# Local attention and two layers on one core: a rational function in two passes, pooled queries by VectorE, larger packets, and Strassen's products in every group of layer two

## The chip, the cores and the metric

The kernel runs on one core of a Trainium2 chip. The metric is the device time of one execution in microseconds (us), the median over several runs; less is better. A core has five engines that work through their own queues: TensorE (PE, with its weight loads listed apart as PEld), VectorE (DVE), ScalarE (ACT), GpSimd (POOL) and SyncE (SP), from which this kernel issues all of its DMAs. Matrix products end in PSUM, eight banks of 512 float32 columns per partition; everything else lies in SBUF.

## The reference, cut to what matters

Attention over 2 x 8 heads of 576 positions and 64 columns has two parts that are added: a coarse one over means of four neighbours (144 positions), and a local one in which a position sees its neighbours at a distance under 4. Its result, 1152 tokens of 512 columns, passes through two layers of width 2048, and all is float32 in accuracy.

```python
q_d = q.reshape(B, H, Sd, factor, D).mean(axis=3)      # k_d, v_d alike, factor = 4
out_up = np.repeat(sm_attn(q_d, k_d, v_d), factor, axis=2)
out_local = softmax(scale * q @ k.T where |i - j| < factor) @ v
x = out_up + out_local                                  # as 1152 x 512

h = x @ w_in                                            # layer one: a rational function
P = a[0] + a[1] * h + a[2] * h**2 + a[3] * h**3
Q = 1.0 + abs(b[0]) * abs(h) + abs(b[1]) * h**2
x = (P / (Q + 1e-06)) @ w_out

h = x @ w_in2                                           # layer two: h * tanh(softplus(h))
return (h * np.tanh(log1p(exp(h)))) @ w_out2
```

The weights come as float64, 8 bytes an element, 32 pieces of 1 MB in all.

## The kernel before

Nothing in it is issued by hand: every piece of work is a task with a cost for each engine that may do it, a priority (a due time in us of planned PE time) and the buffers that it takes and uses. `Plan.run` plays the tasks through a model of the engines and writes each engine's queue in the order that comes out. `SECOND`, `FILL`, `LEAD`, `CLEAD`, `LLEAD`, `OLAG`, `PROL`, `PSTEP`, `VOFF`, `VROFF`, `LOFF` and `KOFF` set due times and when a second engine or a filler matmul (`warm`, L503) is chosen. On the chip each queue runs in that order, held by semaphores.

Attention comes in 18 units (`unit`), each four windows of 64 rows for one pair of heads, and in 8 preparations (`prep`), one for each pair of heads of a batch. `prep` loads keys, transposes them, sums four neighbours (`red`, L572, into kd) and loads values again (`vload`, L584, in runs of 1 KB) for the coarse sums `va` and `vb` (L590, L594). A unit loads queries (L618) and a window of values (L633). `pe_a` transposes the queries (L521) and multiplies them with a matrix `mean` (L645), which gives the pooled queries; `qcopy` (L660) brings both out of PSUM. `pe_b` (L679 to L692) gives the scores, and then come maxima (L704, L705), exponentials (L720, L728), sums (L733), the division (L742, L747), `pe_d` (L758, L763), `copy_p` (L773), `pe_e` (L788, L798), and the result x in two halves: a rounded one `xh` (L837) and the rest `xl` (L842).

Every product of the layers is done as three matmuls of such halves. Layer one works in three groups of 6, 6 and 4 slices of 128 hidden columns. A step is two slices for one chunk of tokens: four chunks in the first group, three of 384 (`TW`) in the others. It does H (L1113), 24 matmuls into two banks. ACT then makes three passes over H out of PSUM, `i_c` (L1133), `i_a` (L1138) and `i_b` (L1141); DVE makes `d_1` (L1148), `d_2` (L1151) and `d_3` (L1156). The quotient follows through Ln and Exp and a Newton step in the first group (L1171 to L1185), or through Ln and Sigmoid for pairs of steps in the others (`flush`, L1057 to L1073, and L1165). Then come the halves of g (L1211, L1216) and O (L1250), which sums in PSUM; `evac` adds that to `part` (L1342).

Layer two has four groups of four slices, two grains each, in pieces: "I" is H for one chunk (`plain`, L1489, 24 matmuls), "S" is H for chunks 1 and 2 together by Strassen's seven products (`seven`, L1433, 42 matmuls), and "O" (L1252, 18 matmuls) follows for a chunk. In the first group all three chunks are "I"; in the others chunk 0 is "I" and the rest "S". "S" needs sums of x (`sums`, L1291, with halves by `halves`, L1268 and L1273) and combinations of the weights: `combine` (L1027), `hi7` (L1031) and `lo7` (L1036), whose result lies in `late_r`, over memory that layer one's last groups use as well. Products p1 and p2 need neither sums nor combined weights.

Weights are decoded from float64 by `scale` (L969) and `low` (L976) on ACT and `join` (L983), `sign` (L989) on DVE, then split by `hi` (L995, L997) and `lo` (L1000). The float32 copy lies in one of two work tiles `wt` until the last of these, `lo7` included, is done.

```python
if m == 1 and kind == "i" and 2 * f >= GROUPS[1][0]:
    w7 = Buf(wT_s)
    ...
    y = add({"dve": 4 * t_dve(256)}, combine, c, after=[x], use=[src], port=True)
    y = add({"act": t_act(2 * DM), "dve": ...}, hi7, c, after=[y] + att_done, take=[w7], use=[src], ...)
```

## Time and profile before

| | |
|---|---|
| median of 3 runs | 487.15 us (486.61 to 492.02) |
| the profiled execution | 486.43 us |
| its span, from the first to the last instruction | 484.7 us |
| PE busy | 475.9 us, 98% |
| DVE busy | 361.2 us, 75% |
| ACT busy | 352.5 us, 73% |
| POOL busy | 55.8 us, 12% |
| HBM read and written | 44.17 MB and 2.36 MB |

The profile is one execution. Attention and layer one's first group fill about the first 130 us, layer one's other groups go on to some 300 us, and layer two ends it. Engine times are shares of the span, and matmuls are pipelined, so that a busy PE can still be waiting; how many matmuls stand in a stretch says more. The chain of waits follows the work that ended last back to the start, at each step to what released it. A wait for several semaphores is put down to the one that came last.

### The profile page before, as it was taken

The page shows a single profiled execution, that of the slowest core. Times are in us where ns is not written, and L with a number is a line of the kernel's source. Part 1 is how long each engine was busy: PE and PEld are TensorE (multiplying, and loading weights), DVE is VectorE, ACT ScalarE, POOL GpSimd, SP SyncE. Part 2 cuts the span into 40 slices and gives each one's busy share as a digit, 9 for nine tenths or more (in the row PEclk, how much of TensorE's full clock was granted, in tenths as well). Part 3 has the DMA queues.
Part 4 walks back from the last instruction along what each step waited for, and adds up shares of the span by engine and source line. Part 5 has one row for each costly group of instructions (what it writes and reads, how often), then busy time and mean ns, then how long its engine had stood idle before and what let it go on. Part 6 is the DMA issues. An engine that isn't in the chain of part 4 may idle for free.

```text
span 484.7 us, 9704 instructions
## 1 busy us (share of the span) xinstructions
PE 475.9 (98%) x4003; PEld 436.8 (90%) x4003; DVE 361.2 (75%) x528; ACT 352.5 (73%) x546; POOL 55.8 (12%) x79
## 2 busy tenths in 40 slices
PE   9989999999999999989999999999999999999996
PEld 5668898899999999989999999898988898889885
DVE  5647989985999988979799997909597759633332
ACT  6678989985899999999799977737667446422320
POOL 1835344644000000000000000000000000000000
PEclk9999999999999999999999999999999999999999
DMA  9868698741024024240312212120505220000103
GB/s 185 196 167 198 177 267 216 202 118 44 1 87 175 1 88 174 87 174 0 101 74 88 87 39 68 68 87 4 171 4 170 88 87 2 0 1 0 66 0 130
DMA packets 47132, 47.16 MB, mean 97 GB/s; under 512 B 30576, under 2 KB 33648, under 8 KB 47088
## 3 DMA queue, kind: packets, MB, share of 16 engines
q1 hardware_dynamic: 47088, 46.54, 32.8%
q8 instruction: 31, 0.51, 0.4%
q14 instruction: 13, 0.11, 0.1%
HBM read 44.17 MB, written 2.36 MB: 96 GB/s over the span
## 4 chain that ended last, share of the span: by engine, by line
PE 93%; ACT 4%; DMA 1%; SPq 1%; DVE 0%; issue 0%; ACTq 0%
PE psum L1250 20%; PE psum L1252 20%; PE psum L1113 20%; PE psum L1489 10%; PE psum L1433 9%; PE psum L503 2%; PE psum L798 2%; PE psum L521 2%; PE psum L686 2%; PE psum L692 1%; PE psum L788 1%; PE psum L645 1%; DMA att<-in_q_dram 1%; PE psum L758 1%; PE psum L763 1%; PE psum L679 1%
## 5 line engine op out<-in xcount | busy, mean ns | idle before, releaser
L1113 PE MATMUL psum<-xh,wi 128*128 128x384 f32 (+1 forms) x336 | 83.8, 320 | 1.2 <-ACT late_f L1141 1.2
L1250 PE MATMUL psum<-gg,wo 128*128 128x384 f32 (+1 forms) x456 | 71.9, 311 | 0.0
L1250 PEld LDWEIGHTS psum<-gg,wo 128*128 128x128 f32 x456 | 68.6, 189 | 0.5 <-ACT raw L976 0.2
L1113 PEld LDWEIGHTS psum<-xh,wi 128*128 128x128 f32 x336 | 59.1, 189 | 2.8 <-ACT late_f L1141 1.6
L1113 PE MATMUL psum<-xl,wi 128*128 128x384 f32 (+1 forms) x168 | 52.4, 312 | 0.0
L1252 PE MATMUL psum<-wo,late_g 128*128 128x512 f32 x216 | 51.6, 391 | 0.0
L1252 PE MATMUL psum<-wo,gg 128*128 128x512 f32 x216 | 51.6, 390 | 0.0
L1489 PE MATMUL psum<-xh,wi 128*128 128x384 f32 x192 | 50.9, 336 | 0.0
L1252 PEld LDWEIGHTS psum<-wo,gg 128*128 128x128 f32 x216 | 40.4, 188 | 8.1
L1252 PEld LDWEIGHTS psum<-wo,late_g 128*128 128x128 f32 x216 | 40.4, 188 | 8.1
L969 ACT ACTIVATE wt<-raw 128x1024 f32<-128x1024 f32 x32 | 36.5, 1144 | 10.1 <-DVE wo L1000 3.9
L983 DVE SCALAR_TENSOR_TENSOR wt<-wt,raw 128x1024 int32<-128x1024 int32 x32 | 39.1, 1223 | 5.9 <-ACT wt L969 4.4
L976 ACT ACTIVATE raw<-raw 128x1024 int32<-128x1024 uint16 x32 | 36.6, 1152 | 5.6 <-DMA raw<-in_moe_w_in_dram 5.5
L1489 PEld LDWEIGHTS psum<-xh,wi 128*128 128x128 f32 x192 | 34.9, 188 | 0.7 <-ACT wrk L1499 0.4
L1489 PE MATMUL psum<-xl,wi 128*128 128x384 f32 x96 | 32.1, 335 | 0.0
L1113 PEld LDWEIGHTS psum<-xl,wi 128*128 128x128 f32 x168 | 31.8, 189 | 0.0
L1499 ACT ACTIVATE wrk<-psum 128x768 f32<-128x768 f32 x10 | 8.0, 814 | 29.6 <-PE psum L1489 29.6
L1365 DVE TENSOR_TENSOR part<-psum,part 128x512 f32<-128x512 f32 x27 | 17.8, 687 | 13.6 <-PE psum L1252 13.6
L1000 DVE TENSOR_TENSOR wi<-wt,wi 128x1024 fp32r<-128x1024 f32 x14 | 17.5, 1258 | 13.5 <-ACT wi L995 13.3
L1113 PE MATMUL psum<-xh,late_r 128*128 128x384 f32 x96 | 25.5, 335 | 0.0
L1057 ACT ACT_TABLE_LOAD x17 | 21.8, 1283 | 0.3
L1000 DVE TENSOR_TENSOR wo<-wt,wo 128x1024 fp32r<-128x1024 f32 x14 | 17.1, 1224 | 5.6 <-ACT wo L995 5.6
(163 smaller groups left out, 1035.5 us busy)
## 6 DMA issues: line engine op xcount, KB each, us to landing
raw<-in_moe_w_in_dram SPq DMA_DIRECT2D x16, 1024.0 KB, 5.5
raw<-in_moe_w_out_dram SPq DMA_DIRECT2D x16, 1024.0 KB, 4.9
att<-in_v_dram SPq DMA_DIRECT2D x64, 48.0 KB, 3.5
out_dram<-part SPq DMA_DIRECT2D x9, 256.0 KB, 2.1
att<-in_q_dram SPq DMA_DIRECT2D x16, 128.0 KB, 5.1
att<-in_k_dram SPq DMA_DIRECT2D x6, 288.0 KB, 3.7
att<-in_v_dram SPq DMA_DIRECT2D x6, 256.0 KB, 7.0
wrk<-in_k_dram SPq DMA_DIRECT2D x2, 288.0 KB, 5.3
```

What stands on the lines that cost most here:

```text
L503: nc.tensor.matmul(view[:, :480], blank[:, :128], blank, start=True, stop=True)
L969: nc.scalar.activation(out=t.v, in_=words(r)[:, :, 1].bitcast(F32), func=AF.Prelu if fold else AF.Identity, scale=2.0 ** -112, **({"alpha" ...
L976: nc.scalar.activation(out=words(r)[:, :, 0], in_=r.v.bitcast(U16).rearrange("p (n four) -> p n four", four=4)[:, :, 1], func=AF.Copy, sca ...
L983: nc.vector.scalar_tensor_tensor(out=ti, in0=ti, scalar=3, in1=words(r)[:, :, 0], op0=ALU.logical_shift_left, op1=ALU.bitwise_or)
L1000: ENG[e].tensor_tensor(out=w.v[:, 1], in0=s.v, in1=w.v[:, 0].bitcast(F32), op=ALU.subtract)
L1057: nc.scalar.preload_act_table_set(name)
L1113: nc.tensor.matmul(st.h.v[:, i, :T], w.v[:, ww, ks], xx[:, kk, c0:c0 + T], start=(nn == 0 and (st.big or i == 0)), stop=(nn == 3 * KD - 1 ...
L1250: nc.tensor.matmul(A(d)[:, :T], w.v[:, ww, lo + d * 128:lo + (d + 1) * 128], vw(gg)[:, i, :], start=start, stop=stop)
L1252: nc.tensor.matmul(A(d), vw(gg)[:, i, sl], w.v[:, ww, lo:lo + DM], start=start, stop=stop)
L1365: nc.vector.tensor_tensor(out=pv, in0=acc.v[:, j], in1=pv, op=ALU.add)
L1433: nc.tensor.matmul(dst.v[:, :TW], wv.v[:, ww, at:at + 128], x(h, kk), start=bool(take) and nn == 0, stop=nn == 5, skip_group_check=not take,)
L1489: nc.tensor.matmul(h.v[:, i, :TW], w.v[:, ww, at:at + 128], xx[:, kk, c0:c0 + TW], start=nn == 0, stop=nn == 3 * KD - 1)
```

## The change

- The mean matmuls go. `pe_a` only transposes, `qcopy` brings 256 columns out of PSUM, and a new DVE operation `qsum` sums each four of them out of PSUM. The factor 1/16 and the scale move to kd, by one more DVE operation for each pair of heads.
- The coarse values are loaded as eight rows for each partition and head, in runs of 2 KB. Halves of the coarse positions are now even and odd, and `red` writes kd in that order.
- The rational function is divided by its leading coefficient once (`leading`, on DVE; the other coefficients in `cf`), and `evac` multiplies by it. ACT makes two passes, Square and Abs. `d_1` is (h^2 + A1) h, `d_3` adds A2 h^2 to it, `d_2` forms the denominator.
- In layer two's first group chunks 1 and 2 are "S" too, in the order I, I, O, O on chunk 0, then S, S, then the O of the other chunks. Weights of all grains are combined. The halves of the third sum of x are made with the others, and the halves of x that nothing reads any more are dropped.
- Ten constants of the planner change. Priorities of loads move: for the coarse values from -3 to -1 of the unit's, for window values from +2 to +1, for queries from -9 to -7, for keys from -11 to -12. Units of the first chunk are 3.0 apart, not 1.5, and those of later chunks come 38 ahead, not 34.

```diff
@@ -21,13 +21,14 @@
-SECOND = 1.6
+EDGE, LEAST = 2.0 ** -60, 1e-30
...
+SECOND = 2.0
...
-WINDOW, FILL, FILL_END = 3.4, 0.7, 450.0
-LEAD, CLEAD, LLEAD, OLAG = 34, 12, 40, 16
-PROL, PSTEP, VOFF, VROFF, LOFF, KOFF = -45, 1.5, 2, -3, 9, 11
+WINDOW, FILL, FILL_END = 3.4, 0.8, 450.0
+LEAD, CLEAD, LLEAD, OLAG = 38, 14, 40, 18
+PROL, PSTEP, VOFF, VROFF, LOFF, KOFF = -45, 3.0, 1, -1, 7, 12
@@ -305,9 +306,9 @@
-    mean = const.tile([128, 64], F32, name="mean")
...
+    cf = const.tile([128, 12], F32, name="cf")
@@ -465,12 +466,6 @@
-    def means():
-        nc.vector.tensor_reduce(
-            out=mean, in_=ident.rearrange("p (s two) -> p s two", two=2), axis=AX.X, op=ALU.add
-        )
-        nc.vector.tensor_scalar(out=mean, in0=mean, scalar1=1.0 / 16.0, scalar2=None, op0=ALU.mult)
@@ -492,11 +487,32 @@
-    t_mn = add({"dve": 0.35}, means, -890, after=[t_id])
...
-    t_b = add({"act": 0.15}, lambda: nc.scalar.activation(out=b_sb, in_=b_sb, func=AF.Abs), -30, after=[t_ab])
+    A0, A1, A2, A3 = (cf[:, i:i + 1] for i in range(4))
+    S0, S1 = (cf[:, i:i + 1] for i in range(4, 6))
...
+    def tiny(out, in_, s1, op0, s2=None, op1=None):
+        kw = {} if op1 is None else {"op1": op1}
+        nc.vector.tensor_scalar(out=out, in0=in_, scalar1=s1, scalar2=s2, op0=op0, **kw)
...
+    def absolute():
+        nc.scalar.activation(out=b_sb, in_=b_sb, func=AF.Abs)
+        nc.scalar.activation(out=cf[:, 8:12], in_=a_sb, func=AF.Abs)
...
+    def leading():
...
+        nc.vector.tensor_reduce(out=S0, in_=cf[:, 8:12], axis=AX.X, op=ALU.max)
+        tiny(S0, S0, EDGE, ALU.mult, LEAST, ALU.max)
+        nc.vector.tensor_tensor(out=S0, in0=S0, in1=cf[:, 11:12], op=ALU.max)
+        tiny(S1, a_sb[:, 3:4], 0.0, ALU.is_ge, 2.0, ALU.mult)
+        nc.vector.scalar_tensor_tensor(out=A3, in0=S1, scalar=-1.0, in1=S0, op0=ALU.add, op1=ALU.mult)
+        nc.vector.reciprocal(out=S0, in_=A3)
+        tiny(cf[:, 0:3], a_sb[:, 0:3], S0, ALU.mult)
...
+    t_b = add({"act": 0.25}, absolute, -30, after=[t_ab])
+    t_b = add({"dve": 0.6}, leading, -30, after=[t_b])
@@ -570,20 +586,21 @@
-                out=kd[p], in_=kT[p].rearrange("c (s f) -> c s f", f=4), axis=AX.X, op=ALU.add
-            )
...
-        kv_done[p] = add({"dve": 0.67}, red, prio, after=copies)
+                out=kd[p].rearrange("c (t s) -> c s t", t=2), in_=kT[p].rearrange("c (s t f) -> c s t f", t=2, f=4), axis=AX.X, op=ALU.add
+            )
+            nc.vector.tensor_scalar(out=kd[p], in0=kd[p], scalar1=SCALE / 16.0, scalar2=None, op0=ALU.mult)
...
+        kv_done[p] = add({"dve": 0.67 + t_dve(SD, True)}, red, prio, after=copies)
...
-            src = v[bb, 2 * p:2 * p + 2].rearrange("h (t p f) d -> p (h t) (f d)", t=2, f=4)
-            dst = vr.v.rearrange("p x f d -> p x (f d)")
+            src = v[bb, 2 * p:2 * p + 2].rearrange("h (p x) d -> p h (x d)", x=8)
+            dst = vr.v.rearrange("p (h t) f d -> p h (t f d)", h=2)
...
-        m0 = add({"sp": 1.25}, vload, prio + VROFF, take=[vr], chain="vr", dma=[(0.65, 1.21), (0.6, 0.16)])
+        m0 = add({"sp": 1.25}, vload, prio + VROFF, take=[vr], chain="vr", dma=[(0.65, 0.8), (0.6, 0.12)])
@@ -641,31 +658,29 @@
-            for r in range(2):
-                nc.tensor.matmul(
-                    qp.v[:, 2 * n:2 * n + 64], qn.v[:, 2 * D * r:2 * D * (r + 1)], mean, start=(r == 0), stop=(r == 1)
-                )
...
-        ta = add({"pe": 0.82}, pe_a, prio, after=[l0, t_id, t_mn], take=[qp, qT] + mix, use=[qn], chain="pa")
...
+        ta = add({"pe": 0.3}, pe_a, prio, after=[l0, t_id], take=[qp, qT] + mix, use=[qn], chain="pa")
...
-            ops = [(qT.v, qp.v[:, :320])]
+            dst, src = qT.v[:, :256], qp.v[:, :256]
+            if e == "act":
+                nc.scalar.activation(out=dst, in_=src, func=AF.Identity, scale=SCALE)
+            else:
+                nc.vector.tensor_scalar(out=dst, in0=src, scalar1=SCALE, scalar2=None, op0=ALU.mult)
...
+        def qsum():
+            dst, src = qT.v[:, 256:320], qp.v[:, :256].rearrange("c (s f) -> c s f", f=4)
...
-                ops = [
-                    (qT.v[:, :256], qp.v[:, :256]),
-                    (qx.v[:, :, :16], qp.v[:, 256:320].rearrange("c (w s) -> c w s", w=4)),
-                ]
-            for dst, src in ops:
-                if e == "act":
-                    nc.scalar.activation(out=dst, in_=src, func=AF.Identity, scale=SCALE)
-                else:
-                    nc.vector.tensor_scalar(out=dst, in0=src, scalar1=SCALE, scalar2=None, op0=ALU.mult)
+                dst, src = qx.v[:, :, :16], qp.v[:, :256].rearrange("c (w s f) -> c w s f", w=4, f=4)
+            nc.vector.tensor_reduce(out=dst, in_=src, axis=AX.X, op=ALU.add)
...
-        ex_ = 0.2 if mixed else 0
-        tq = add({"act": t_act(320, True) + ex_, "dve": t_dve(320) + ex_}, qcopy, prio, after=[ta, t_cd], use=[qp, qT] + mix)
+        tq = [
+            add({"act": t_act(256, True), "dve": t_dve(256)}, qcopy, prio, after=[ta], use=[qp, qT]),
+            add({"dve": t_dve(256)}, qsum, prio, after=[ta, t_cd], use=[qp, qT] + mix),
+        ]
@@ -882,7 +897,8 @@
-            order = [(w, c, j) for c in range(3) for w in "IO" for j in js]
+            order = [("I", 0, j) for j in js] + [("O", 0, j) for j in js] + [("S", 1, j) for j in js]
+            order += [("O", c, j) for c in (1, 2) for j in js]
@@ -1016,7 +1032,7 @@
-        if m == 1 and kind == "i" and 2 * f >= GROUPS[1][0]:
+        if m == 1 and kind == "i":
@@ -1129,41 +1145,37 @@
-        def i_c():
-            nc.scalar.activation(
-                out=vw(st.c), in_=H(), func=AF.Identity, bias=a_sb[:, 2:3], scale=a_sb[:, 3:4]
-            )
...
-            nc.scalar.activation(out=vw(st.a), in_=H(), func=AF.Abs)
+            nc.scalar.activation(out=vw(st.a), in_=H(), func=AF.Square)
...
-            nc.scalar.activation(out=vw(st.b), in_=H(), func=AF.Abs, scale=b_sb[:, 1:2])
...
-        tc_ = add({"act": t_act(n, True, 2)}, i_c, pr, after=th + [t_b], take=[st.c], use=[st.h], chain="ic")
+            nc.scalar.activation(out=vw(st.b), in_=H(), func=AF.Abs, scale=b_sb[:, 0:1])
...
-            nc.vector.tensor_tensor(out=vw(st.c), in0=vw(st.c), in1=H(), op=ALU.mult)
+            nc.vector.scalar_tensor_tensor(
+                out=vw(st.c), in0=vw(st.a), scalar=A1, in1=H(), op0=ALU.add, op1=ALU.mult
+            )
...
-                out=vw(st.b), in0=vw(st.b), scalar=b_sb[:, 0:1], in1=vw(st.a), op0=ALU.add, op1=ALU.mult
-            )
...
-        def d_3():
-            nc.vector.scalar_tensor_tensor(
-                out=vw(st.c), in0=vw(st.c), scalar=a_sb[:, 1:2], in1=H(), op0=ALU.add, op1=ALU.mult
-            )
...
-        t1 = add({"dve": t_dve(n)}, d_1, pr, after=[tc_], use=[st.c, st.h])
-        t3 = add({"dve": t_dve(n, ptr=1)}, d_3, pr, after=[t1], use=[st.c, st.h])
+                out=vw(st.b), in0=vw(st.a), scalar=b_sb[:, 1:2], in1=vw(st.b), op0=ALU.mult, op1=ALU.add
+            )
...
+        def d_3(e="dve"):
+            ENG[e].scalar_tensor_tensor(
+                out=vw(st.c), in0=vw(st.a), scalar=A2, in1=vw(st.c), op0=ALU.mult, op1=ALU.add
+            )
...
+        t1 = add({"dve": t_dve(n, ptr=1)}, d_1, pr, after=[ta, t_b], take=[st.c], use=[st.a, st.h], chain="ic")
...
+        t3 = add({"dve": t_dve(n, ptr=1)}, d_3, pr, after=[t1], use=[st.a, st.c], port=True)
@@ -1187,7 +1199,7 @@
-            tr = add({"act": 2 * t_act(n, ptr=1) + 0.05 + 0.15 * st.big}, act_r, pr, after=[t2, t_bias], use=[st.a, st.b])
+            tr = add({"act": 2 * t_act(n, ptr=1) + 0.05 + 0.15 * st.big}, act_r, pr, after=[t2, t3, t_bias], use=[st.a, st.b])
@@ -1303,10 +1315,8 @@
-        def third(after):
-            sums_done[3] = halves(lambda: xh[at], lambda: xl[at], lambda: vw(three), n, pr + 10, [t3] + after, use=[three])
...
-        sums_done.update({1: h1, 2: h2, 4: h4, "raw": [t1, t2, t3, t4], "third": third})
+        h3 = halves(lambda: xh[at], lambda: xl[at], lambda: vw(three), n, pr + 10, [t3], use=[three])
+        sums_done.update({1: h1, 2: h2, 3: h3, 4: h4, "raw": [t1, t2, t3, t4]})
@@ -1329,22 +1339,22 @@
-                            nc.scalar.activation(out=pv, in_=av(), func=AF.Identity)
+                            nc.scalar.activation(out=pv, in_=av(), func=AF.Identity, scale=A3)
...
-                    nc.vector.tensor_tensor(out=pv, in0=av(), in1=pv, op=ALU.add)
...
+                    nc.vector.scalar_tensor_tensor(out=pv, in0=av(), scalar=A3, in1=pv, op0=ALU.mult, op1=ALU.add)
...
-                if st.final:
+                if st.final and (c0, d) != (2 * TW, 0):
@@ -1411,7 +1421,7 @@
-        x1, x2 = x2_done[TW], x2_done[2 * TW]
+        x1, x2 = x2_done[TW], x2_done[2 * TW][-2:]
@@ -1468,7 +1478,7 @@
-        p4 = prod(A, cols(1, 1), x2[2:], 1, 1, 0, [c22])
+        p4 = prod(A, cols(1, 1), x2, 1, 1, 0, [c22])
@@ -1499,19 +1509,15 @@
-        if st.gi == 1 and 3 not in sums_done:
-            sums_done["third"](old)
```

## Rows read from the trace of the kernel before

**Rows 1.** The page: busy time by engine; TensorE's granted clock in 40 slices.

```profile
PE 475.9 (98%) x4003; PEld 436.8 (90%) x4003; DVE 361.2 (75%) x528; ACT 352.5 (73%) x546; POOL 55.8 (12%) x79
...
PEclk9999999999999999999999999999999999999999
```

**Rows 2.** Stretches: busy us (count) of PE, PEld, DVE, ACT, POOL; clock, DMA.

```profile
36.00:132.00 96.00, 95.70 (x1606) 86.13 (x1605) 81.36 (x160) 82.67 (x190) 40.09 (x49) 1.00 0.59 155
...
132.00:203.00 71.00, 70.99 (x427) 70.46 (x426) 67.17 (x75) 69.41 (x82) 0.00 (x0) 1.00 0.29 104
...
203.00:212.50 9.50, 8.27 (x48) 7.94 (x46) 7.61 (x9) 9.44 (x11) 0.00 (x0) 1.00 0.51 172
```

**Rows 3.** Chain of work that ended last, off PE: start us, us, what.

```profile
29.92 5.56 DMA att<-in_q_dram
...
43.04 0.78 ACT wrk L1133
...
52.80 0.47 PE psum L521 x3
...
202.98 0.99 ACT late_f L1133
...
211.66 0.80 ACT late_f L1141
```

**Rows 4.** The same chain: one group of three kinds of matmuls.

```profile
67.27 0.39 PE psum L645 x4
...
302.65 8.20 PE psum L1252 x36
...
321.16 8.34 PE psum L1489 x48
```

**Rows 5.** One stretch, matmuls and weight loads of L645 alone; columns likewise.

```profile
52.80:122.00 69.20, 4.45 (x32) 4.20 (x32) 1.00 0.60 159
```

**Rows 6.** Groups by line and shape, 0 to 130 us: busy, mean ns.

```profile
L704 DVE TENSOR_REDUCE att<-psum 128x4 f32<-128x192 f32 x18 | 6.3, 349 | 4.4 <-PE psum L692 4.2
...
L705 DVE TENSOR_REDUCE att<-psum 128x1 f32<-128x144 f32 x18 | 5.3, 297 | 0.0
...
L1133 ACT ACTIVATE wrk<-psum,a_sb 128x512 f32<-128x512 f32 x9 | 7.0, 773 | 0.4 <-PE psum L1113 0.4
...
L1148 DVE TENSOR_TENSOR wrk<-wrk,psum 128x512 f32<-128x512 f32 x8 | 5.4, 681 | 4.2 <-ACT wrk L1141 4.2
...
L1156 DVE SCALAR_TENSOR_TENSOR wrk<-wrk,a_sb,psum 128x512 f32<-128x512 f32 x8 | 5.9, 734 | 0.0
...
L1180 DVE SCALAR_TENSOR_TENSOR wrk<-wrk,a_sb 128x512 f32<-128x512 f32 x7 | 6.1, 867 | 0.0
```

**Rows 7.** The same, 132 to 300 us.

```profile
L1151 DVE SCALAR_TENSOR_TENSOR late_f<-late_f,b_sb,wrk 128x768 f32<-128x768 f32 x14 | 14.2, 1012 | 0.3 <-ACT late_f L1141 0.3
...
L1156 DVE SCALAR_TENSOR_TENSOR late_f<-late_f,a_sb,psum 128x768 f32<-128x768 f32 x10 | 10.1, 1008 | 0.0
```

**Rows 8.** The page, DMA issues: KB each, median us from issue to landing.

```profile
raw<-in_moe_w_in_dram SPq DMA_DIRECT2D x16, 1024.0 KB, 5.5
...
att<-in_v_dram SPq DMA_DIRECT2D x6, 256.0 KB, 7.0
```

**Rows 9.** Timeline of DVE and ACT, 281 to 313 us: start, duration.

```profile
281.12 1.80 DVE L1027 TENSOR_TENSOR wt<-wt 128x256 f32<-128x256 f32 x4
...
293.20 1.06 ACT L1031 ACTIVATE late_r<-wt 128x1024 fp32r<-128x1024 f32 x1
...
296.67 1.14 ACT L969 ACTIVATE wt<-raw 128x1024 f32<-128x1024 f32 x1
...
300.24 1.81 DVE L1342 TENSOR_TENSOR part<-psum,part 128x768 f32<-128x768 f32 x2
...
308.05 1.22 DVE L1000 TENSOR_TENSOR wo<-wt,wo 128x1024 fp32r<-128x1024 f32 x1
...
312.06 0.95 DVE L1273 TENSOR_TENSOR late_r<-wrk,late_r 128x768 fp32r<-128x768 f32 x1
```

More of the change, by code (lines that the diff above doesn't have):

```diff
@@ L695, in unit @@
             {"pe": 1.77 if mixed else 1.04}, pe_b, prio,
-            after=[tq] + [kv_done[p] for p in pairs] + [t_i16, t_mk[kind]],
+            after=tq + [kv_done[p] for p in pairs] + [t_i16, t_mk[kind]],
             take=[sc, tm, s, pd],
@@ L1511 @@
         elif st.what == "I":
[L1512 to L1514 removed]
+            gs[st.gi, st.ci, st.j] = plain(st)
         else:
```

17 lines of the change are left out of this document (7 added, 10 removed).

## The prediction

> **What bounds the kernel now.** I read the page first: TensorE (PE) is busy for 98% of the span at the full granted clock, 1.00, which is the 2.4 GHz level [rows 1]. Matmuls are pipelined, so "busy" alone does not say that PE is the limit. The stretches say more [rows 2]. From 132 to 203 us PE does 427 matmuls in 71.0 us, one per 166 ns, while from 203 to 212.5 us there are only 48 in 9.5 us. The chain of waits names what ends last in each part [rows 3]. Three regimes follow from it:
>
> - 0 to 53 us: the chain leaves PE for a transfer of queries (5.56 us from 29.92) and, from 43.04 to 52.80, for one ScalarE (ACT) instruction after another, the pass L1133 among them. Here latencies set the pace and PE fills holes with dummy matmuls.
> - 53 to 203 us: every step of the chain is PE, one queue worked off without a hole. VectorE (DVE) is close behind: 81.4 of 96 us between 36 and 132, 67.2 of 71.0 after that [rows 2].
> - 203 to the end: PE again, but for one hole at 203 to 212.5 us, whose chain runs on ACT from a pass L1133 to a pass L1141 [rows 3].
>
> So a matmul taken out after 53 us is worth its own duration, provided that DVE, to which the change hands work, still keeps up.
>
> **Strassen's products in layer two's first group.** Before, each of the group's two grains computes chunks 1 and 2 with two plain pieces of 24 matmuls, 48 in all. After, one piece "S" of 42 does it, so 12 matmuls go. A row of 48 such matmuls takes 8.34 us, 0.174 us each [rows 4]. **-2.1 us**, in a stretch where the chain is all PE. What it needs is costed below, under the boundary.
>
> **The mean matmuls.** One unit of attention (there are 18) loses four matmul records at L645, 0.39 us on the chain [rows 4]. By the stretches, 8 units have theirs between 52.8 and 122 us (32 records) [rows 5], the other 10 earlier. Only the 8 lie where PE alone sets the pace: 8 x 0.39 = **-3.1 us**. The bounds are nothing (DVE takes over) and all 18, 7.0 us (each unit's start-up latency also ends on PE). I take 3.1, since filler and waits stand in the first regime.
>
> **Two ACT passes instead of three.** L1133 goes: 27 instructions, 0.77 us with 512 columns and about 0.99 with 768 [rows 3, 6]. Most of it lies beside a dense PE and is worth nothing there. It is worth something twice. One instruction of 0.78 us stands on the chain at 43.04: **-0.8 us** (bounds: nothing, and 1.5 for a second one). And at 203 to 212.5 us PE lacks about 9 matmuls (9.5 us at 71.0/427 would be 57, 48 are there) [rows 2], 9 x 0.174 = 1.6 us. ACT works through that hole without rest (9.44 of 9.50 us), the chain begins there with L1133 itself, and matmul buffers come free only after the last pass that reads them, L1141. A pass fewer per step removes more than the hole: **-1.5 us** (bounds nothing and 1.6). Also, d_3 now reads the square from SBUF and no longer the matmul's bank, so banks come free after Square, Abs and d_1.
>
> **What DVE gets.** qsum reduces 256 columns out of PSUM. Reduces of 192 and 144 columns take 349 and 297 ns [rows 6], so 1.08 ns a column and about 0.42 us here; 18 of them, of which some 12 lie between 36 and 132 us: 5.0 us. The scaling of kd (144 columns): at most the 0.297 us of a reduce of that width, with nothing as the lower bound; I take 0.22, nearer to the row, for six in that stretch: 1.3 us. d_1 becomes a scalar_tensor_tensor, 734 instead of 681 ns: 9 x 0.05 = 0.5 us. d_3 has two SBUF inputs and no PSUM input: the two-SBUF L1180 takes 867 ns where L1156 takes 734 [rows 6]: 9 x 0.13 = 1.2 us. Sum 8.0 us, against 96.0 - 81.4 = 14.6 us idle [rows 2]. If the stretch shortens by 3.9 us as well (mean matmuls and the pass), 2.7 us of slack remain in 92, which a queue with dependencies will not use wholly. ACT, in exchange, loses 9 x 0.77 us there. I charge **+1.0 us**, a quarter of the 3.9; the bounds are nothing and all 3.9. Behind a late qsum waits pe_b of that unit, behind that L704 and the whole softmax. In layer one's later groups POOL rests and L1156 (1008 ns) already equals the two-SBUF L1151 (1012) [rows 7]: only the pointer scalar in d_1 and in the evacuations is left, 0.06 us each, beside PE. leading's seven tiny operations and ACT's second Abs come once, at no more than the 0.3 us of L705 each, and end before the first H is read at 43.04.
>
> The price of d_3 is where the Trainium skill (GPSIMD Engine Reference, section 1, Specifications) speaks against the change: it says that GpSimd shares its SBUF interfaces with VectorE and that they contend when a VectorE instruction has two SBUF inputs. The trace agrees while GpSimd works (867 against 734 ns [rows 6]) and shows equal times once it rests [rows 7]. By a price without that rule d_3 would cost nothing more and the sum would fall by a part of 1.2 us; I keep the rows' price.
>
> **Coarse values in 2 KB runs.** The same 288 KB per pair, in half as many packets. 256 KB of it took 7.0 us to land, where a megabyte of weights took 5.5 [rows 8], so there is something to win; but what waits for it is GpSimd's sum, and the chain has no such wait. I take nothing; the bounds are nothing and 1.5 us, the DMA wait before the query tile of 29.92 in the first regime. Issues and queue stay the same, two per pair, at priorities shifted by a few us; a moved issue can delay a query behind it on SP by one issue of some 0.6 us in the first regime, inside the same bound.
>
> **The boundary between the layers.** Here work moves forward. Strassen's sums of x now feed the first group, not the second, and two more grains need combine, hi7 and lo7 (1.80 us on DVE, 1.06 on ACT, and on DVE again 1.22, as L1000 of the same size). The last addition of layer one starts at 300.24 and the last low half of a sum ends at 313.0: 12.8 us, with decoding of weights in between [rows 9]. PE's cover for it is O on chunk 0, 36 matmuls in 8.20 us [rows 4], and products p1 and p2, 12 x 0.174 = 2.1 us, which need no sum. p5, the first that does, needs only the first sum, and each next product (1.04 us) one more. h3 is added (0.95 us), one x2 half pair is dropped. So the bounds are nothing and 12.8 - 8.2 - 2.1 = 2.5 us; I charge **+0.5 us**, near the lower one, since the sums come one product ahead of their use. The worse case is a rival below.
>
> **Sum.** The profiled execution took 486.43 us (span 484.7 plus 1.7 around it), and the median of the runs is 487.15. -2.1 -3.1 -0.8 -1.5 +1.0 +0.5 = -6.0, so 480.4; I predict **480.5 us**, its own range 477.5 to 482.5.
>
> **Rivals.** (a) DVE becomes the bound up to 132 us. For it: 2.7 us slack as worked out above, and 67.2 of 71.0 us busy right behind, so that a backlog has no place to go. Against it: ACT is relieved, and half of the added work is short. The mean matmuls and the first ACT gain are then lost, and the charge for DVE with them: 486.4 - 2.1 - 1.5 + 0.5 = 483.3, and up to a microsecond more: 484. (b) Slower than before: a grain's float32 copy stays in one of two work tiles until hi7 finds room in late_r. Before, one such copy waited from 282.9 (end of combine) to 293.2, and the next grain's scale stood at 296.67 [rows 9]. If the first group's grains hold both tiles until layer one's last O ends (T), the weights of O on chunk 0 are decoded only then: 1.06 + 1.22 for hi7 and lo7, then 1.14 for scale, 3 x 1.22 for join, sign and lo (L1000's size) and 1.06 for hi, 5.9 together: T + 8.2. PE has p1 and p2 for 2.1 us of that: a hole of 6.1. The sums share DVE with it (a second grain's 3.7 more): about 10 in all, 480.5 + 9.9 = 490.4. It turns the change into a loss once the hole exceeds 6.6 us. Against it: late_r's part for g comes free several times before the end, and hi7, now with an early due time, can take it then. (c) More: all 18 units' 7.0 us and the 1.5 of DMA count, 480.5 - 3.9 - 1.5 = 475.
>
> **How the numbers follow.** Forecast 0.50, (a) 0.25, (b) 0.12, (c) 0.13. The range leaves out most of (b) and a part of (c): 475.5 to 488. A measurement of this kernel tells about 1% from no change; 1% below the median is 482.3. Faster by more: 0.46 of the forecast and 0.12 of (c), 0.58. Slower by more (above 492): the tail of (b), 0.07. Within 1%: 0.35.
>
> **What would show it.** Layer two has 528 instead of 540 matmuls in pieces I and S; the hole at 203 is gone; no L645 group, and PE reaches layer one's second group some 4 us earlier, with DVE above 92% busy up to there. A PE hole that ends on a DVE reduce before 130 us shows (a); one that ends on wo right after layer one's last O shows (b). I am wrong in kind if the gain comes from the first 53 us, or if a new PE hole stands behind DVE in layer one's later groups.

## The result, and the profile after

The changed kernel takes 484.23 us in the median of 18 runs (481.59 to 486.70), the kernel before 488.27 in 18 runs beside it: a ratio of 0.9903, interval 0.9878 to 0.9929. The profiled execution took 484.05 us (span 482.3) against 486.43. The forecast was 480.5 with a range of 475.5 to 488.0. So the time lies in the range and the sign was right. The range held by its width: 484.23 lies outside the forecast's own 477.5 to 482.5, and on the price of rival (a), 484. Of the 6 us that the sum promised, the ratio gives 4.7 (3.5 to 6.0 by its interval) and the profiled pair 2.4. The pair is the lowest reading: over the runs whose mean granted clock is 0.998 or more the medians are 483.33 us (9 of the changed kernel's 18) and 487.45 (56 of the 96 runs of the kernel before that stand beside the experiments), 4.1 us apart. The rest of this text is about where the remainder stayed.

The page of the changed kernel; the last line is the chain that ended last, by engine. Line numbers are now those of the changed kernel.

```profile
PE 472.1 (98%) x3944; PEld 429.2 (89%) x3944; DVE 381.1 (79%) x569; ACT 340.6 (71%) x531; POOL 58.0 (12%) x80
...
PEclk9999999999999999999999999999999999999999
...
PE 85%; DVE 4%; ACT 4%; DMA 4%; SPq 2%; issue 1%; POOL 0%; ACTq 0%; POOLq 0%
```

Against [rows 1] DVE has 20 us more, ACT 12 less, PE 59 matmuls less. Of PE's the exact make-up can be read: 72 for the means and 12 for Strassen went, and 25 fillers came. Of the 25, 18 stand before 53 us (64 fillers against 46), where the prediction gave the mean matmuls no worth, and 7 behind it.

Fillers over the whole span (matmuls of L503 before, of L519 after: count | busy us, mean ns | idle before), first the kernel before, then the changed one:

```profile
L503 PE MATMUL psum<-blank 128*128 128x480 bf16 x49 | 13.5, 405 | 1.2 <-DVE band L488 1.2
```

```profile
L519 PE MATMUL psum<-blank 128*128 128x480 bf16 x74 | 20.2, 400 | 1.2 <-DVE band L483 1.2
```

Stretches of the changed kernel: busy us (count) of PE, PEld, DVE, ACT, POOL, then granted clock and DMA share.

```profile
0.00:132.00 132.00, 127.50 (x2087) 103.34 (x2088) 115.26 (x264) 102.05 (x243) 58.02 (x80) 1.00 0.67 162
...
36.00:132.00 96.00, 94.27 (x1548) 82.77 (x1547) 90.84 (x184) 79.19 (x180) 40.04 (x48) 1.00 0.62 154
...
132.00:203.00 71.00, 71.00 (x427) 71.00 (x426) 67.81 (x73) 64.35 (x74) 0.00 (x0) 1.00 0.32 105
203.00:235.00 32.00, 32.00 (x186) 32.00 (x186) 26.84 (x30) 25.29 (x27) 0.00 (x0) 1.00 0.19 66
235.00:245.50 10.50, 8.73 (x51) 8.41 (x50) 9.14 (x10) 10.19 (x12) 0.00 (x0) 1.00 0.58 200
```

The same first stretch of the kernel before:

```profile
0.00:132.00 132.00, 128.38 (x2128) 108.56 (x2129) 101.31 (x229) 106.28 (x252) 55.80 (x79) 1.00 0.65 163
```

Two readings. The dense part runs as before, 427 matmuls in 71.0 us [rows 2], so but for holes what is left to do at 132 us fixes the end. Before, 4003 - 2128 = 1875 matmuls were left; now 3944 - 2087 = 1857. Twelve of these 18 are Strassen's, so the whole work on attention, on ACT and on the means gave a lead of 6 matmuls, some 1.0 us, in this execution. At 53 us there was no lead at all: without means, fillers and Strassen's twelve, 3113 matmuls were left in both (3160 - 32 - 3 - 12 and 3123 - 10). One execution says little here, though: e2, e9 and e12 below keep the changed kernel's order of PE up to 132 us, and counted likewise they lead by 17, 12 and 16 matmuls there, 2.1 to 3.0 us. And the hole of 203 to 212.5 us [rows 2] is gone from there and stands at 235 to 245.5, larger: 1.77 us of PE idle where it was 1.23. The ledger of the profiled pair: 12 x 0.174 = 2.1 for Strassen, 1.0 up to 132 us, -0.5 for the hole, 2.6 together, against 2.4 measured.

The chain of the changed kernel up to 98 us, its longest pieces off PE (start us, us, what):

```profile
19.37 8.48 DMA att<-in_q_dram
...
33.42 4.24 DMA att<-in_q_dram
...
45.45 6.15 DMA att<-in_q_dram
...
82.20 1.06 DVE att L749
...
91.92 1.89 DVE wo L1016
...
95.11 1.17 DVE wrk L1163
```

Before, one such query load of 5.56 us stood on the chain [rows 3]; now three do, 18.9 us together, and the chain is off PE again and again until 98 us, where it was all PE from 52.80 on. The last piece of it, 80.35 to 98.25 us, is DVE for 12.8 us and ACT for 4.6, and DVE has hardly a pause there:

```profile
80.00:98.00 18.00, 18.00 (x289) 15.07 (x287) 17.59 (x36) 16.51 (x40) 11.65 (x12) 1.00 0.72 175
```

In e9, the same order, the chain is all PE in that stretch. So the chain of one execution doesn't tell which engine sets the pace; DVE is near its limit there, and 7 of PE's matmuls are fillers.

The waits of PE over 1 us in the changed kernel (total, times, longest):

```profile
PE psum L537 <- DMA att<-in_q_dram: 2.7, 3, 1.5
PE psum L1129 <- ACT late_f L1152: 1.8, 1, 1.8
PE psum L519 <- DVE band L483: 1.2, 1, 1.2
```

### The profile page after: what moved, and what is told of

It is laid out like the page before. It is cut to its first block, busy times and chain, and to the rows that moved or that the text cites. A ratio compares the mean times of both kernels' runs of the same rounds, so it can differ in the third digit from the quotient of the medians.

```text
span 482.3 us, 9623 instructions
## 1 busy us (share of the span) xinstructions
PE 472.1 (98%) x3944; PEld 429.2 (89%) x3944; DVE 381.1 (79%) x569; ACT 340.6 (71%) x531; POOL 58.0 (12%) x80
## 4 chain that ended last, share of the span: by engine, by line
PE 85%; DVE 4%; ACT 4%; DMA 4%; SPq 2%; issue 1%; POOL 0%; ACTq 0%; POOLq 0%
PE psum L1264 20%; PE psum L1262 20%; PE psum L1129 18%; PE psum L1443 12%; PE psum L1499 7%; DMA att<-in_q_dram 4%; PE psum L519 2%; PE psum L537 1%; PE psum L813 1%; PE psum L803 1%; PE psum L707 1%; PE psum L701 1%; SPq L650 1%; DVE wo L1016 1%; ACT L1073 1%
## 5 line engine op out<-in xcount | busy, mean ns | idle before, releaser
L1129 PE MATMUL psum<-xh,wi 128*128 128x384 f32 (+1 forms) x336 | 82.4, 318 | 2.0 <-ACT late_f L1152 1.8
L1262 PE MATMUL psum<-gg,wo 128*128 128x384 f32 (+1 forms) x480 | 75.9, 312 | 0.0
L1262 PEld LDWEIGHTS psum<-gg,wo 128*128 128x128 f32 x480 | 72.7, 189 | 0.6 <-issue 0.5
L1129 PEld LDWEIGHTS psum<-xh,wi 128*128 128x128 f32 x336 | 58.7, 189 | 3.7 <-ACT late_f L1152 2.1
L1499 PE MATMUL psum<-xh,wi 128*128 128x384 f32 x128 | 34.4, 335 | 0.0
L1149 ACT ACTIVATE wrk<-psum 128x768 f32<-128x768 f32 (+1 forms) x27 | 19.8, 735 | 8.3 <-PE psum L1129 8.0
L1011 ACT ACTIVATE wo<-wt 128x1024 fp32r<-128x1024 f32 x13 | 13.8, 1061 | 16.0 <-DVE wt L1005 7.6
L1499 PEld LDWEIGHTS psum<-xh,wi 128*128 128x128 f32 x128 | 23.3, 188 | 0.2
L1499 PE MATMUL psum<-xl,wi 128*128 128x384 f32 x64 | 21.4, 335 | 0.0
```

What stands on the lines that cost most here:

```text
L1129: nc.tensor.matmul(st.h.v[:, i, :T], w.v[:, ww, ks], xx[:, kk, c0:c0 + T], start=(nn == 0 and (st.big or i == 0)), stop=(nn == 3 * KD - 1 ...
L1149: nc.scalar.activation(out=vw(st.a), in_=H(), func=AF.Square)
L1262: nc.tensor.matmul(A(d)[:, :T], w.v[:, ww, lo + d * 128:lo + (d + 1) * 128], vw(gg)[:, i, :], start=start, stop=stop)
L1499: nc.tensor.matmul(h.v[:, i, :TW], w.v[:, ww, at:at + 128], xx[:, kk, c0:c0 + TW], start=nn == 0, stop=nn == 3 * KD - 1)
```

## The experiments

The theories when they began. **Parts**: each part is worth its own term. **Pace of VectorE**: DVE, 90.84 of 96 us busy, sets the pace up to 132 us, so that the mean matmuls were worth nothing. **Order**: ten constants of the planner came with the diff, and the order that they write suits one set of parts; a part that is changed without them costs or hides more than its own price. Each ratio is against the kernel before, on the same chip. The last columns are of the profiled execution: matmuls left at 132 us (the page's count less that of the first stretch), fillers, and the us of the span at the lower clock of 0.50, as stretches of 2 us show them.

| kernel | median us | ratio, interval | span | left at 132 | fillers | at 0.50 |
|---|---|---|---|---|---|---|
| before (profile) | 487.15 | 1 | 484.7 | 1875 | 49 | none |
| changed | 484.23 | 0.9903, 0.9878 to 0.9929 | 482.3 | 1857 | 74 | none |
| e1 mean matmuls back | 494.12 | 1.0105, 1.0068 to 1.0142 | 489.9 | 1909 | 56 | none |
| e2 plain first group | 485.68 | 0.9953, 0.9924 to 0.9982 | 483.4 | 1858 | 74 | none |
| e3 three passes | 490.64 | 1.0050, 1.0022 to 1.0078 | 488.7 | 1901 | 101 | none |
| e4 old constants | 488.22 | 0.9978, 0.9945 to 1.0010 | 484.2 | 1873 | 90 | none |
| e5 before, new constants | 495.91 | 1.0113, 1.0066 to 1.0159 | 494.3 | 1947 | 76 | 63 to 70 |
| e6 means back, refitted | 488.37 | 0.9972, 0.9939 to 1.0006 | 488.8 | 1907 | 43 | 56 to 63 |
| e7 three passes, refitted | 486.17 | 0.9940, 0.9910 to 0.9970 | 486.1 | 1874 | 90 | 60 to 63 |
| e8 kd scaled on ACT, refitted | 484.64 | 0.9917, 0.9882 to 0.9952 | 482.5 | 1857 | 76 | none |
| e9 old packets | 484.25 | 0.9907, 0.9870 to 0.9944 | 482.4 | 1851 | 74 | 246 to 249 |
| e10 passes first | 489.73 | 1.0011, 0.9974 to 1.0048 | 489.0 | 1903 | 83 | 58 to 64 |
| e11 measured prices | 491.90 | 1.0068, 1.0037 to 1.0098 | 489.4 | 1911 | 108 | 30 to 33 |
| e12 passes first, last group only | 481.15 | 0.9869, 0.9833 to 0.9904 | 479.6 | 1847 | 74 | none |

From 132 us to the end every one of them takes 0.186 to 0.189 us per matmul left (482.3 - 132 over 1857 is 0.1886; e5, 362.3 over 1947, 0.1861). A straight line through the fourteen points (0.134 us for each matmul left, since not all are of one size) meets every span to within 1.6 us. So but for a microsecond or two, all differences are made before 132 us.

**Parts undone one by one, the order's constants unchanged.** e1 has the mean matmuls again and neither qsum nor the scaling of kd:

```diff
+            for r in range(2):
+                nc.tensor.matmul(qp.v[:, 2 * n:2 * n + 64], qn.v[:, ...], mean, start=(r == 0), stop=(r == 1))
...
-            nc.vector.tensor_scalar(out=kd[p], in0=kd[p], scalar1=SCALE / 16.0, scalar2=None, op0=ALU.mult)
...
-            add({"dve": t_dve(256)}, qsum, prio, after=[ta, t_cd], use=[qp, qT] + mix),
```

> The changed kernel with the mean matmuls back, and qsum and the scaling of kd on VectorE gone. Theory D (VectorE sets the pace up to about 100 us: it is busy for 90.8 of 96 us between 36 and 132, qsum takes 0.414 us and the scaling 0.408): TensorE gets 18 x 0.39 = 7.0 us of work back, VectorE loses 18 x 0.414 + 8 x 0.408 = 10.7 us, and the time stays within 1.5 us of the changed kernel's or falls by up to 2; VectorE then stands at about 83 of 96 us. Theory P (TensorE sets the pace there, and the missing gain went elsewhere): slower than the changed kernel by the forecast's 3.1 us, ratio to before about 0.997.

Slower than the changed kernel by 1.0105 - 0.9903 = 2.0%, ten microseconds, though the matmuls that came back are 7.0 us in all, and DVE is busy for 16 us less in the first stretch than in the changed kernel (7 us less over the whole span; the rest comes later):

```profile
0.00:132.00 132.00, 125.06 (x2089) 104.02 (x2090) 98.82 (x226) 97.59 (x236) 57.32 (x80) 1.00 0.66 162
```

PE too was idle more (6.9 us against 4.5). A pace set by VectorE alone would have made e1 as fast as the changed kernel; with a less busy DVE it is slower by more than the matmuls' price. But the order's constants are not e1's own, so this is no price of a part; e6 below is the fairer run.

e2 gives layer two's first group its plain pieces again:

```diff
-            order = [("I", 0, j) for j in js] + [("O", 0, j) for j in js] + [("S", 1, j) for j in js]
-            order += [("O", c, j) for c in (1, 2) for j in js]
+            order = [(w, c, j) for c in range(3) for w in "IO" for j in js]
```

> The changed kernel with plain pieces in layer two's first group, as before. All theories: 12 matmuls more, 2.1 us slower than the changed kernel, ratio to before about 0.995. If the boundary between the layers hides a cost of the early sums or of the two more combined grains, less than 1 us slower; the boundary theory in its strong form (weights late): faster than the changed kernel.

0.9953 against 0.9903: 0.5%, 2.4 us (the two intervals' half widths in quadrature are 0.39%, 1.9 us). The forecast's 2.1 agrees.

e3 makes the three passes over H again:

```diff
+        def i_c():
+            nc.scalar.activation(out=vw(st.c), in_=H(), func=AF.Identity, bias=a_sb[:, 2:3], scale=a_sb[:, 3:4])
...
-        t1 = add({"dve": t_dve(n, ptr=1)}, d_1, pr, after=[ta, t_b], take=[st.c], ...)
+        t1 = add({"dve": t_dve(n)}, d_1, pr, after=[tc_], use=[st.c, st.h])
```

> The changed kernel with the rational function of before: three ScalarE passes, no leading coefficient. Forecast's theory (a ScalarE pass is on the path at 43 us and in the hole of TensorE in layer one): 2 to 3 us slower than the changed kernel. Rival (the hole comes from the order on ScalarE, where a pair of Ln and Sigmoid with two table loads stands between the passes of one step, and the passes themselves lie beside a dense TensorE): within 1 us of it. With VectorE as the bound the first 130 us do not change, since d_1 and d_3 together keep their length within 0.1 us.

1.5% slower than the changed kernel, 7 us, more than three times the 2.3 us that were forecast for the pass. Its 44 matmuls more at 132 us explain it, not the later stretches.

e4 is the whole change with the planner's old constants:

```diff
-SECOND = 2.0
-WINDOW, FILL, FILL_END = 3.4, 0.8, 450.0
-LEAD, CLEAD, LLEAD, OLAG = 38, 14, 40, 18
-PROL, PSTEP, VOFF, VROFF, LOFF, KOFF = -45, 3.0, 1, -1, 7, 12
+SECOND = 1.6
+WINDOW, FILL, FILL_END = 3.4, 0.7, 450.0
+LEAD, CLEAD, LLEAD, OLAG = 34, 12, 40, 16
+PROL, PSTEP, VOFF, VROFF, LOFF, KOFF = -45, 1.5, 2, -3, 9, 11
```

> The changed kernel with the ten planner constants of before. If the new due times of loads cost something (the chain of the changed kernel waits for query transfers for 8.48, 4.24 and 6.15 us before 52 us, that of before for 5.56), the time falls by 1 to 3 us. If VectorE is the bound whatever the order, it stays within 1.5 us. If the constants carry the gain, it rises by 2 us or more.

0.9978: with the old order the whole change is worth 0.2%, and can't be told from nothing. The constants, which the prediction passed over, are worth 0.75% (half widths 0.41%), 3.7 us, to these parts.

**Is it the order?** e5 turns e4 round: the kernel before with the new constants, nothing else.

> The kernel before with the ten planner constants of the changed one, nothing else. Theory C (a set of constants fits one combination of parts: the order of some 130 us of attention and layer one's first group hangs on it, and the wrong set costs 3 to 8 us whatever the parts): 3 to 8 us slower than before. Rival (the new constants are better in themselves, since the changed kernel loses 3.7 us with the old ones): 2 to 4 us faster than before.

1.0113: the constants alone make the kernel before slower by 5.5 us, a part of it at the lower clock (63 to 70 us in its profile). So they hold no gain of their own; they suit the changed parts and hurt the old ones. e6 is e1 with two constants moved (`FILL` 0.7, `LLEAD` 43), e7 is e3 with three moved (`LLEAD` 46, `VOFF` 3, `KOFF` 13), each set as the planner's own model of the engines prefers it.

> The changed kernel with the mean matmuls back, qsum and the scaling of kd gone, and two constants chosen for this combination (FILL 0.7 for 0.8, LLEAD 43 for 40). Theory C: most of the 10 us that the same edit cost with unchanged constants comes back, and what is left is the part's own worth, the 3 us of 8 units' TensorE time: ratio to before 0.994 to 0.999. Theory D (VectorE the bound, the mean matmuls worth nothing): as fast as the changed kernel, ratio 0.988 to 0.992. If the part is worth the 7 us of all 18 units: 1.003 to 1.006.

> The changed kernel with the three passes of before and three constants chosen for this combination (LLEAD 46 for 40, VOFF 3 for 1, KOFF 13 for 12). Theory C: of the 7.2 us that the edit cost with unchanged constants about 2 to 3.5 are left, as forecast for the ScalarE pass: ratio 0.994 to 0.998. If the pass is worth all of it: 1.003 to 1.007. If it lies beside a dense TensorE: 0.989 to 0.992.

Two constants bring e1 from 1.0105 to 0.9972, three bring e3 from 1.0050 to 0.9940: 6.5 and 5.4 us, without a change of what is computed. "Order" holds. Against these the changed kernel is ahead by 0.69% (half widths 0.42%), 3.4 us, for the mean matmuls, and by 0.37% (0.39%), 1.8 us, for the third pass, near the forecast's 3.1 and 2.3. Both are upper bounds rather than prices: three constants are no full search, and both profiles hold some microseconds at the lower clock, which the changed kernel's doesn't. e6's runs lie between 485.80 and 491.33; the profiled one, with that clock, took 490.59. The quickest, at a mean granted clock of 0.999, is 2.5 us behind the 483.33 of the changed kernel's runs at 0.998 or more, so that some of the 3.4 is the clock.

**Does VectorE set the pace?** e8 scales kd on ACT, in a task of its own, with `LEAD` 34 and `LOFF` 11:

```diff
-            nc.vector.tensor_scalar(out=kd[p], in0=kd[p], scalar1=SCALE / 16.0, scalar2=None, op0=ALU.mult)
+            nc.scalar.activation(out=kd[p], in_=kd[p], func=AF.Identity, scale=SCALE / 16.0)
```

> The changed kernel with the scaling of kd on ScalarE instead of VectorE (8 instructions of 0.408 us each leave VectorE, about 0.3 us each come on ScalarE), and two constants chosen for it (LEAD 34 for 38, LOFF 11 for 7). Theory D (VectorE sets the pace up to 100 us): 1 to 3 us faster than the changed kernel, ratio to before 0.984 to 0.988, VectorE's share between 36 and 132 us down from 90.8 to about 88. Theory C alone: within 2 us of it either way.

0.9917 and the same 1857 matmuls left: no gain. But in the changed kernel all eight scalings start between 8.8 and 72.5 us, so e8 takes nothing off DVE between 80 and 98 us, where the chain of that execution stands on it. e11 instead gives the planner DVE's measured prices (all 0.07 us dearer, `red` 1.15 in place of 0.98; `VOFF` 0, `VROFF` -2):

```diff
-    return 0.068 + n * (0.000521 if fast else 0.001042) + 0.06 * ptr
+    return 0.14 + n * (0.000521 if fast else 0.001042) + 0.06 * ptr
```

> The changed kernel with the planner's prices of VectorE put to what the trace measured (every VectorE operation 0.07 us dearer, the reduction of the keys with its scaling 1.15 us in place of 0.98), and two constants put to it (VOFF 0, VROFF -2). Theory 'the stretch up to 132 us loses its time because the written order takes VectorE to be quicker than it is, so that TensorE stands at orders it cannot keep': the stretch ends 1 to 3 us earlier, 0.984 to 0.988 of the kernel before. Rival 'VectorE's lateness isn't what the order gets wrong there, since taking 3.3 us off it brought nothing': 0.989 to 0.997, no gain over the changed kernel.

Both expectations missed: it is 1.65% slower than the changed kernel, with 108 fillers and 1911 matmuls left. Its chain has a load of weights at 74.46 us for 8.23 us, which the changed kernel's has not. A truer price of one engine moved all due times and made a worse order. What DVE's lateness costs is thereby not settled. e6, which DVE's pace would have made as fast as the changed kernel and which is slower, speaks against DVE alone as the bound up to 132 us; that it sets the pace between 80 and 98 us is neither shown nor excluded.

**The packets.** e9 has runs of 1 KB, the planner's prices for them as they were, so that no instruction moves:

```diff
-            src = v[bb, 2 * p:2 * p + 2].rearrange("h (p x) d -> p h (x d)", x=8)
+            src = v[bb, 2 * p:2 * p + 2].rearrange("h (t p f) d -> p (h t) (f d)", t=2, f=4)
```

> The changed kernel with the coarse values in the packets of before (eight packets of 1 KB and the reduction that goes with them), everything else, the planner's prices of these transfers among it, as it is, so that the order of every instruction stays the same. The long issue of the coarse values took 7.0 us from issue to landing before and 5.9 us now. Theory 'the packets are worth nothing, because the loads are waited for at no place on the chain' (the forecast's step): 0.990 of the kernel before, within 0.003 of the changed kernel. Rival 'the coarse values are late in the first groups, where the chain now waits for query loads behind the same queue': up to 1.1 us for each of the first three to four loads, so 0.994 to 0.998, and the chain shows waits for the values or for the queries behind them that are longer than in the changed kernel (19.37, 33.42 and 45.45 us there).

0.9907 against 0.9903. The loads of 256 KB land in 5.9 us now (median) where [rows 8] has 7.0, but with the old packets in the same order they take 6.0. So the packets did not make them land sooner, and the chain doesn't wait for them.

**The hole.** The changed kernel's ACT through it, start and duration:

```profile
235.25 0.82 ACT L1149 ACTIVATE wrk<-psum 128x768 f32<-128x768 f32 x1 [1.28 <-PE psum L1129]
...
237.82 1.28 ACT L1073 ACT_TABLE_LOAD   x1
...
240.79 0.79 ACT L1149 ACTIVATE wrk<-psum 128x768 f32<-128x768 f32 x1
241.59 1.28 ACT L1073 ACT_TABLE_LOAD   x1
242.89 0.84 ACT L1089 ACTIVATE wrk<-wrk 128x768 f32<-128x768 f32 x1
243.64 0.83 ACT L1089 ACTIVATE late_f<-late_f 128x768 f32<-128x768 f32 x1
244.37 0.88 ACT L1152 ACTIVATE late_f<-psum,b_sb 128x768 f32<-128x768 f32 x1
```

A step's second pass (L1152), which frees H's banks, stands behind a table load and the flush's two sigmoids, 2.8 us after its first. PE's wait of 1.8 us is for it. e10 gives both passes an earlier due time everywhere, with five constants moved (`SECOND` 1.0, `CLEAD` 16, `LLEAD` 43, `OLAG` 16, `VROFF` -2); e12 does it in layer one's last group alone, with no constant moved, so that up to about 235 us PE's order is that of the changed kernel. The kernel before shows the same thing in its hole at 203 us: the passes of one step, L1133 and then L1138 and L1141, stand 6.9 us apart, with both table loads between them:

```profile
202.98 0.99 ACT L1133 ACTIVATE late_f<-psum,a_sb 128x768 f32<-128x768 f32 x1 [0.18 <-PE psum L1113]
203.99 1.28 ACT L1057 ACT_TABLE_LOAD   x1
...
208.09 1.28 ACT L1057 ACT_TABLE_LOAD   x1
...
210.87 0.79 ACT L1138 ACTIVATE wrk<-psum 128x768 f32<-128x768 f32 x1
211.56 0.89 ACT L1141 ACTIVATE late_f<-psum,b_sb 128x768 f32<-128x768 f32 x1
```

The two edits of e12:

```diff
-        ta = add({"act": t_act(n, True)}, i_a, pr, after=th, take=[st.a], use=[st.h], chain="ia")
-        tb = add({"act": t_act(n, True, 1)}, i_b, pr, after=th + [t_b], take=[st.b], use=[st.h], chain="ib")
+        ta = add({"act": t_act(n, True)}, i_a, pr - (20 if (st.m, st.gi) == (0, 2) else 0), ...)
+        tb = add({"act": t_act(n, True, 1)}, i_b, pr - (20 if (st.m, st.gi) == (0, 2) else 0), ...)
```

> The changed kernel with the two ScalarE passes of the rational function ahead of the flush's logarithm and sigmoid in the list of due times, and five planner constants put to it (SECOND 1.0, CLEAD 16, LLEAD 43, OLAG 16, VROFF -2). Theory 'the hole that moved from 203 us to 235 to 245 us is made by ScalarE's order, two passes with table loads standing between the two passes of one step': PE's idle time in that stretch (1.8 us) goes, nothing comes in its place, and the time is 0.986 to 0.988 of the kernel before. Rival 'ScalarE's work is only shifted, and the hole comes up at another step of layer one or at the start of layer two': 0.989 to 0.993, with a hole of 1 to 2 us elsewhere between 200 and 300 us.

> The changed kernel with the two ScalarE passes ahead of the flush's logarithm and sigmoid in layer one's last group alone, all constants as they are: the order of TensorE's instructions is the same up to its 790th row, about 235 us, and the second pass (L1152) then stands ahead of the table load that it stood behind. The run before this with the passes first everywhere had no idle time of TensorE between 203 and 300 us, but five other constants lost 6 us up to 132 us. Theory 'the hole at 235 to 245 us is ScalarE's order': TensorE's busy time in 203 to 300 us rises from 95.2 to 96.5 or more, everything up to 203 us is as in the changed kernel, and the time is 0.986 to 0.988 of the kernel before. Rival 'the work that ScalarE puts off comes back as another hole behind it, up to the start of layer two': busy time in 203 to 346 us together rises by less than 0.5 us and the time is 0.989 to 0.993.

e10's hole is gone, and the kernel is slower than both its theories said: the time is lost earlier. Stretches of e10 (columns as above):

```profile
56.00:58.00 2.00, 0.49 (x12) 0.37 (x12) 0.02 (x1) 2.00 (x5) 1.32 (x2) 0.94 0.59 63
58.00:64.00 6.00, 6.00 (x57) 5.44 (x56) 4.11 (x7) 4.90 (x14) 2.55 (x3) 0.50 0.86 236
...
203.00:300.00 97.00, 97.00 (x560) 96.89 (x559) 85.92 (x96) 78.78 (x87) 0.00 (x0) 1.00 0.19 63
```

PE has no idle time from 203 to 300 us, but 1903 matmuls were left at 132. Its chain waits for a load of weights from 47.00 for 8.78 us, and PE then runs at the lower clock, 0.50, for some 6 us. e12 keeps the order up to there:

```profile
132.00:203.00 71.00, 71.00 (x426) 71.00 (x425) 67.77 (x73) 64.69 (x73) 0.00 (x0) 1.00 0.31 105
...
235.00:245.50 10.50, 10.50 (x62) 10.25 (x60) 8.82 (x10) 10.44 (x13) 0.00 (x0) 1.00 0.49 192
...
203.00:346.00 143.00, 142.40 (x783) 136.94 (x783) 122.20 (x138) 115.33 (x140) 0.00 (x0) 1.00 0.23 78
```

62 matmuls in the 10.5 us where the changed kernel had 51. From 203 to 346 us PE is busy 142.40 us, against 141.19 in the changed kernel, so 1.2 us came back and stayed (from 203 to 300 us it is busy 96.40 us, a tenth under the 96.5 that was expected). The ratio, 0.9869, is the best of all; its lead over the changed kernel's 0.9903 (0.34%, 1.7 us) is within the half widths (0.44%). Of the 2.7 us between the two spans, 10 matmuls, up to 1.7 us, were ahead at 132 us already, under the same order: that much two executions can differ. That ScalarE's order makes the hole is shown; that e12 is faster than the changed kernel is likely, not settled.

## Why the prediction came out as it did

**Strassen: right.** 2.1 forecast, 2.4 measured in e2, give or take 1.9. The matmul counts agree (528 of I and S).

**The boundary between the layers: right, with a smaller charge.** 0.5 was charged; the chain from 285 to 300 us is PE without a gap (a block O of layer one, a plain piece, an O of layer two), and from 300 to 346 us PE is busy for 46.00 of 46 us. Rival (b), the 10 us hole, did not appear.

**The mean matmuls: the size agrees, the place is not shown.** The weak step is "only the 8 lie where PE alone sets the pace: 8 x 0.39 = 3.1". It took the chain of before as given: all PE from 52.80. In the profiled execution of the changed kernel it is not all PE there, and the stretch up to 132 us got 1.0 us shorter where the mean matmuls, the pass at 43 us and the charge for DVE summed to 2.9. But three other executions of that order lead by 2.1 to 3.0 us, so a shortfall up to 132 us is not settled. With orders fitted to both, 3.4 us at most are the means' (e6). That the time came out at rival (a)'s price does not bear out its reason: (a) has the means worth nothing, and e6 is 2.5 to 3.4 us slower than the changed kernel. The 484.23 and the 484 agree by luck, since (a) counted the hole's 1.5 as a gain.

**The pass at 43 us: gone, and replaced.** L1133 no longer stands on the chain there, but two query loads do, 4.24 us from 33.42 and 6.15 from 45.45. At 53 us the profiled pair had the same work left, so nothing of the 0.8 shows there; "nothing" was the prediction's lower bound. No run moved this pass alone.

**The hole at 203: the step that failed.** "A pass fewer per step removes more than the hole: -1.5 us." The sum counted ACT's work and not its order. Before, the hole's chain began with a pass and ended with one [rows 3], and I read that as three passes being too many. The flush that stands between them was in the trace, and so was the size: PE is idle for 1.23 us of the 9.50 [rows 2], less than the 1.5 and the bound of 1.6. After, two passes with a flush and its table loads between them make the same hole at another step, 0.5 us larger. e12 moves the passes past the flush, and it goes. With +0.5 in place of -1.5 the sum is -4.0, which is what the runs at full clock show (4.1) and lies in the interval of the ratio (3.5 to 6.0): this one term is enough for the shortfall, though others may have missed in both directions.

**DVE's load: right in sum, wrong in its parts.** It rose from 81.36 to 90.84 us in 36 to 132, 9.5 where 8.0 were forecast, 94.6% busy. Groups of the changed kernel from 0 to 130 us, busy and mean ns:

```profile
L675 DVE TENSOR_REDUCE att<-psum 128x64 f32<-128x256 f32 x18 | 7.4, 414 | 4.7 <-PE psum L537 4.6
...
L1163 DVE SCALAR_TENSOR_TENSOR wrk<-wrk,b_sb 128x512 f32<-128x512 f32 x8 | 7.1, 893 | 0.0
L1158 DVE SCALAR_TENSOR_TENSOR wrk<-wrk,cf,psum 128x512 f32<-128x512 f32 x9 | 6.6, 736 | 0.3 <-ACT wrk L1152 0.3
L1168 DVE SCALAR_TENSOR_TENSOR wrk<-wrk,cf 128x512 f32<-128x512 f32 x8 | 5.9, 740 | 0.0
```

qsum took 414 ns (418 forecast), d_1 736 (734). d_3 (L1168) took 740, not 867: its eight lie between 735 and 745 ns, so GpSimd stretched none of them. That is the order's doing: only two of the eight overlap a GpSimd instruction, by 0.1 us each. d_2 (L1163), with two SBUF tensors as well, runs from 714 to 1256 ns, and the longest lies beside three GpSimd instructions. The scaling of kd, forecast at 220, has this line (min, median, max):

```profile
L591 DVE TENSOR_SCALAR att<-att x8: 234/286/1202, 8.8 to 72.5; 128x144 f32<-128x144 f32 x8
```

**The packets: right**, nothing (e9).

**What was left out of the sum.** The constants. They were ten numbers in the diff with no instruction behind them, and the prediction costed instructions. Without them 3.7 us of the 4.7 are gone and the other parts are worth 0.2% together (e4); without the parts they cost 5.5 us (e5). What stays open is what holds PE up between 53 and 98 us: the chain of the changed kernel names DVE and ACT, that of e9 PE, and that of e12 a load of values and GpSimd behind it, all in one order, and no experiment took one of these away alone.

## What to carry to other kernels

When a planner writes the order, a part's worth can't be read by undoing it alone: an unsuited order costs more (here 3.7 to 6.5 us) than the part (2 to 3). Refit the order for each variant, judge the refit on the chip, and count the work left at the point where the dense part starts, which here told every kernel's time to within 2 us. Profile an order more than once before a lead of a microsecond is read from it: here the same order differed by 11 matmuls, up to 1.9 us, at that point. And when a chain through one engine makes a hole, read the order of that engine's instructions in it before its sum.
